# Attention with beacons and a max-out layer: the opening's steps in a new order

## The chip, the cores and the metric

The kernel runs on one core of one Trainium2 chip. That core has five engines, each with a program of its own that it works through in order: TensorE (PE in the profile; its weight loads have a row of their own, PEld), VectorE (DVE), ScalarE (ACT), GpSimd (POOL) and SyncE (SP). [...] Transfers between the device memory and the on-chip memory are issued by an instruction on SP, ACT or POOL and then run by themselves on 16 DMA engines; SP's and ACT's are called hardware-generated in the profile (queues q1 and q10), POOL's software-generated (q0). The metric is the device time of one execution in microseconds (us); lower is better.

## What is computed

Attention for 8 batches and 8 heads over 576 tokens with 64 values per head, with 16 beacon keys and values put in front of every head, and then a feed-forward layer with the maximum of three products:

```
k_all = concatenate([beacon_k, k]); v_all = concatenate([beacon_v, v])
scores = (q @ k_all.T) / sqrt(64)        # causal over the 576 tokens, beacons always seen
a = softmax(scores); x = a @ v_all       # heads side by side: 4608 tokens x 512
h = max(x @ w1, x @ w2, x @ w3)          # 512 x 768 each
out = h @ w_out                          # 768 x 512
```

## The kernel before

**Pairs, quads, halves.** The 64 heads of all batches are handled as 32 pairs; a batch has four (pairs 0 to 3 are batch 0). Two pairs make a quad: quad 0 is pairs 0 and 1, quad 1 is pairs 2 and 3. For batch 0 the 576 tokens are also cut in two halves of 288, so that the first half can be loaded, turned and used before the second is there.

**What a pair goes through.** Its q and k are loaded with tokens on the partitions, cast to bf16, turned on PE by transposes against an identity (`turn_half`, line 428, transposes in line 440; `turn` for whole pairs, lines 384 to 402), and copied from PSUM into `qT` and `kT` (line 448, or `evac_q` and `evac_k`, lines 452 to 467). The beacon keys of batch 0 are loaded apart ("load keys 0", line 351), cast (line 864), turned (`turn_beacons`, line 356) and copied into the first 16 columns of `kT`: for pair 0 directly (line 366), for all pairs by way of `bT` (line 367), from which "keys" (`place_beacons`, line 460) copies them for one pair. "scores p g" (`emit_scores`, line 503) issues the products of one of four groups of key tiles (line 514) and one ACT exponential over all of them (line 523). "mask p g" zeroes what lies above the diagonal, on POOL by an affine select (line 542) or on DVE by a product with a triangle (line 540). "values quad half" (`emit_pv`, line 561) multiplies with a column of ones and with v (line 583); "invert" and "multiply" divide by the sums (lines 604, 606 and 616) and write `xT`.

**The feed-forward part.** "ffn" (`mm1_halves`, line 634) multiplies a block of `xT` with one of the three weights, 8 matmuls of 256 columns (line 638), and DVE takes the result, by a copy for the first weight (line 630) and by a maximum for the others (line 632). In the opening the weights are used in their order, three steps each: the first three "ffn" steps with last argument 0 need the first weight, the next three the second, the last three the third. Each weight is loaded by POOL in two DMAs that cast on the way ("load w", line 338), the first with the rows for quad 0, the second with those for quad 1.

**Loads of the first batch.** Pairs 0 and 1, first half: q and k apart, from SP or ACT as the list says ("load half", line 223), cast by an engine (line 231). Pairs 2 and 3, first half, and all second halves: by POOL with a cast on the way, two pairs at once ("load quad half", line 240; `("load quad half", 1, 0)` is pairs 2 and 3, first half, `(0, 1)` pairs 0 and 1, second half). "load quad" does the same for pairs 4 to 7 (line 249), "load pair" loads pairs 8 and 9 by SP. "load v0 t" (line 298) loads tile t of batch 0's v by SP; where an engine is named, that engine first writes one word of the tile (line 301), so that SP can't issue the load before that engine has come so far. "cast v0 t" casts it (line 328).

**Filler.** PE runs matmuls of no use in three forms: "busy n cols" (`keep_busy`, line 482) n matmuls of a constant tile; the last argument of "scores" and "values" (`spare`, line 476) so many of 320 columns ahead of the step; the last two arguments of "half" (`fill`, line 404) so many pairs of transposes ahead of the turn, in the order idle for k, then idle_q for q. All are in PE's program, so they take their time even if the step behind them could go ahead.

**The order of the work** is written out by hand in two lists, `first_steps` (lines 901 to 1074) and `loop_steps` (from line 1075), which are emitted one after the other. Every step issues its instructions, DMAs too, to the end of the programs of the engines that it uses. `first_steps` handles batch 0 and most of batch 1; `loop_steps` the rest.

## Time and profile before

| What | Value |
|---|---|
| Time, median of three runs (lowest to highest) | 285.1 us (284.79 to 286.19) |
| The profiled execution's own time | 285.21 us |
| Its span, first to last instruction | 283.3 us |
| PE busy | 276.3 us, 98% of the span |
| DVE, ACT, POOL busy | 176.5, 154.5, 143.4 us |
| Loaded and stored | 35.13 MB read, 9.44 MB written |

The time of an execution is 1.9 us longer than its span; that part lies before the first and behind the last instruction. A busy PE is not a PE that does useful work: filler counts as busy. The page's chain of waits follows the end of the execution back to its start; the tables by stage show how busy each engine is in a stretch of time; the timeline lists instructions in order of start with the idle time before them and what ended it; the list of DMA issues tells for each how long it took from issue to landing.

### The profile page before, as it was taken

To read this page: it belongs to the slowest core of one execution; us is meant where nothing else is said; L and a number is where in the kernel's file an instruction comes from. 1 tells how busy PE (TensorE), PEld (TensorE's weight loads), DVE (VectorE), ACT (ScalarE), POOL (GpSimd) and SP (SyncE) were. 2 spreads that over 40 slices of the span, in tenths; PEclk is the share of its full clock that TensorE was granted. 3 is DMA by queue.
4 is the path that set the end of the run, shared out by engine and by line. 5 is a ranking of instruction groups with operands and counts; after the bars stand their busy time and mean duration, and the time that the engine had idled before them with its cause. 6 is when DMAs were issued, how large, how long until landed. Compare 5 with 4: busy or idle time off the path is not lost.

```text
span 283.3 us, 11781 instructions
## 1 busy us (share of the span) xinstructions
PE 276.3 (98%) x5099; PEld 201.5 (71%) x5099; DVE 176.5 (62%) x331; ACT 154.5 (55%) x249; POOL 143.4 (51%) x316
## 2 busy tenths in 40 slices
PE   8999999999999999999999999999999999999995
PEld 7666777757777576768677686767877687757762
DVE  2456777886676765756566666646575665661754
ACT  2876676897563574637464574725765474624000
POOL 4462318898741583758734497508854682400000
PEclk9999999999999999999999999999999999999999
DMA  9999999999978399999999969989999962003004
GB/s 153 168 171 206 223 234 157 247 206 309 211 141 168 45 252 178 171 197 147 189 178 215 236 91 176 166 204 185 217 160 170 163 177 76 2 3 150 2 2 185
DMA packets 118307, 46.27 MB, mean 163 GB/s; under 512 B 107248, under 2 KB 112880, under 8 KB 118256
## 3 DMA queue, kind: packets, MB, share of 16 engines
q1 hardware_dynamic: 111888, 39.20, 75.6%
q0 software_dynamic: 5808, 6.00, 13.0%
q8 instruction: 40, 0.66, 1.1%
q10 hardware_dynamic: 560, 0.33, 0.4%
q14 instruction: 11, 0.09, 0.1%
HBM read 35.13 MB, written 9.44 MB: 157 GB/s over the span
## 4 chain that ended last, share of the span: by engine, by line
PE 91%; DMA 3%; ACT 2%; POOL 1%; DVE 1%; issue 1%; ACTq 0%; POOLq 0%
PE t L700 44%; PE t L726 16%; PE t L583 11%; PE t L514 6%; DMA quad<-in_k_dram 3%; PE pv L478 2%; ACT at_sb L523 2%; PE pv L638 2%; PE sc L514 1%; PE sc L638 1%; PE fps L638 1%; PE t L398 1%; POOL at_sb L542 1%; PE wide L583 1%; PE pv L583 1%
## 5 line engine op out<-in xcount | busy, mean ns | idle before, releaser
L700 PE MATMUL t<-xT,w_sb 64*128 64x288 bf16 (+1 forms) x1008 | 129.6, 285 | 0.0
L700 PE MATMUL t<-xC,wC 64*128 64x288 bf16 (+1 forms) x1008 | 129.6, 285 | 0.0
L523 ACT ACTIVATE at_sb<-t 128x992 bf16<-128x992 f32 (+1 forms) x96 | 82.6, 863 | 42.8 <-PE t L514 37.1
L632 DVE TENSOR_TENSOR hT<-hT,t 128x576 bf16<-128x576 bf16 (+1 forms) x84 | 63.7, 763 | 30.6 <-PE t L700 30.6
L542 POOL TENSOR_SCALAR_AFFINE_SELECT at_sb<-at_sb 128x256 bf16<-128x256 bf16 (+2 forms) x143 | 53.6, 390 | 53.7 <-ACT at_sb L523 41.2
L700 PEld LDWEIGHTS <-w_sb 64*128 64x128 bf16 x1008 | 51.3, 94 | 12.6 <-issue 1.1
L700 PEld LDWEIGHTS <-wC 64*128 64x128 bf16 x1008 | 51.0, 94 | 12.4
L726 PE MATMUL t<-w_out_sb,hT 128*128 128x512 bf16 x210 | 47.9, 380 | 0.0
L681 POOL COPY xC<-xT 64x576 bf16<-64x576 bf16 (+1 forms) x26 | 18.0, 693 | 42.8 <-DVE xT L616 42.5
L630 DVE CAST hT<-t 128x576 bf16<-128x576 f32 (+1 forms) x36 | 27.7, 769 | 14.8 <-PE t L700 14.6
L726 PEld LDWEIGHTS <-hT 128*128 128x128 bf16 x210 | 19.3, 98 | 22.8 <-issue 0.9
L259 POOL CAST p<-st 96x768 bf16<-96x768 f32 x44 | 34.9, 822 | 0.3
L734 DVE COPY y<-t 128x1024 f32<-128x1024 f32 (+1 forms) x20 | 21.8, 1091 | 20.5 <-PE t L726 20.3
L514 PE MATMUL t<-qT,kT 64*128 64x288 bf16 (+4 forms) x288 | 33.1, 279 | 0.0
L616 DVE TENSOR_TENSOR xT<-t,recip 128x288 bf16<-128x288 f32 (+2 forms) x78 | 22.9, 351 | 16.0 <-ACT recip L606 10.7
L604 ACT ACTIVATE lnd<-t 128x288 f32<-128x288 f32 x26 | 10.7, 410 | 36.9 <-PE t L583 36.9
L514 PEld LDWEIGHTS <-kT 64*128 64x128 bf16 x400 | 18.5, 94 | 11.4 <-issue 6.7
L583 PEld LDWEIGHTS <-v_sb 128*32 128x32 bf16 (+1 forms) x1408 | 24.6, 96 | 1.6 <-issue 0.4
L523 ACT ACTIVATE at_sb<-sc 128x736 bf16<-128x736 f32 (+5 forms) x28 | 23.2, 862 | 4.2 <-PE sc L514 4.1
L583 PE MATMUL t<-at_sb,v_sb 128*32 128x96 bf16 (+8 forms) x1144 | 23.3, 228 | 0.0
L316 POOL CAST v_sb<-st 128x1536 bf16<-128x1536 f32 (+2 forms) x21 | 18.4, 894 | 0.6 <-DMA st<-in_v_dram 0.6
L583 PEld LDWEIGHTS <-ones 128*32 128x32 bf16 (+2 forms) x512 | 10.9, 95 | 6.7 <-issue 3.9
(125 smaller groups left out, 220.1 us busy)
## 6 DMA issues: line engine op xcount, KB each, us to landing
out_dram<-y SPq DMA_DIRECT2D x15, 512.0 KB, 4.6
st<-in_q_dram SPq DMA_DIRECT2D x24, 288.0 KB, 5.8
st<-in_k_dram SPq DMA_DIRECT2D x24, 288.0 KB, 6.2
st<-in_v_dram SPq DMA_DIRECT2D x24, 256.0 KB, 5.5
w_sb<-in_moe_w_dram POOLq DMA_DIRECT2D x6, 384.0 KB, 8.9
st<-in_v_dram SPq DMA_DIRECT2D x8, 224.0 KB, 5.1
st<-in_v_dram SPq DMA_DIRECT2D x8, 160.0 KB, 4.7
out_dram<-y SPq DMA_DIRECT2D x5, 256.0 KB, 4.6
```

What stands on the lines that cost most here:

```text
L259: cast(t16.rearrange("p r h d -> p h r d"), st[0:QP, i * NQ2 : (i + 1) * NQ2].rearrange("p (h r d) -> p h r d", h=2, r=QR),)
L316: cast(v_sb[0:n, t:t1].rearrange("p t h d -> p (t h d)"), st[0:n, (t - t_lo) * H * D : (t1 - t_lo) * H * D],)
L514: nc.tensor.matmul(ps[:, e, off : off + q1 - q0], kT[hs, 128 * t : 128 * t + 128], qT[hs, q0:q1], start=True, stop=True, tile_position=(64 ...
L523: nc.scalar.activation(out=both_heads(p, gi), in_=ps[:, :, 0 : g_width(p, gi)], func=AF.Exp, scale=scale)
L542: nc.gpsimd.affine_select(out=view, in_=view, compare_op=ALU.is_ge, fill=0.0, base=x0, pattern=[[0, 2], [1, hi - lo]], channel_multiplier=-1,)
L583: nc.tensor.matmul(ps[bank][32 * j : 32 * j + 32, lo + q0 - qa : lo + qb - qa], lhsT, at_view(PPQ * quad + j // 2, t, j % 2, q0, qb), star ...
L616: nc.vector.tensor_mul(xT[:, 2 * g + part - 1, c0 + ca : c0 + cb], ps[bank][:, lo : lo + cb - ca], recip[:, ca:cb],)
L630: (by_i or by_dve)(h, ps)
L632: nc.vector.tensor_max(h, h, ps)
L700: nc.tensor.matmul(ps[:, e], w[own(e), ct, cols], x, start=(ct == 0 and not over), stop=(ct == n_ct - 1 and over), tile_position=(64 * e, 0),)
L726: nc.tensor.matmul(ps[:, u], h_tile(tt + u, ft), w_out_sb[:, ft, :], start=(ft == 0), stop=(ft == n_ft - 1),)
L734: nc.vector.tensor_copy(y[:, 0:n], ps[:, 0:n])
```

## The change

Only `first_steps` changes; every function and the whole of `loop_steps` stay. Every operation on data is still done, once. What differs is the order, the queue or engine of some steps, and the filler:

- q of pair 0 goes from SP to ACT, q of pair 1 from ACT to SP. ACT's queue issues q of pair 0, the beacon keys, k of pair 0 and k of pair 1, in this order. SP's issues q of pair 1 alone.
- The first filler is 40 matmuls of 64 columns and 12 of 174, instead of 27 of 200 and 16 of 160.
- The triangle is made later, behind the first beacon copy on POOL.
- PE turns pair 0, the beacon keys, pair 3 and then pair 1, where it turned the beacon keys, pair 0, pair 1, pair 3; scores of pair 1 come first, then pair 0, pair 2, pair 3.
- Casts, masks and beacon copies go to other engines in many places, and the later loads by POOL and SP stand at other places in the order.

The diff, with its core; what is left out moves steps of the same kinds between the places shown:

```
 first_steps = [
-    ("load half", 0, 0, "sp"),
-    ("busy", 27, 200),
+    ("load half", 0, 0, "act"),
+    ("load keys 0", "act"),
     ("identity",),
-    ("busy", 16, 160),
-    ("triangle",),
+    ("load half", 0, 1, "act"),
     ("load quad half", 1, 0),
-    ("load half", 1, 0, "act"),
-    ("load half", 0, 1, "act"),
-    ("cast half", 0, 1, "dve"),
-    ("load keys 0", "act"),
+    ("busy", 40, 64),
+    ("busy", 12, 174),
+    ("load half", 1, 0, "sp"),
+    ("load half", 1, 1, "act"),
+    ("cast half", 0, 0, "dve"),
+    ("cast half", 0, 1, "act"),
     ("cast keys 0", "act"),
-    ("load half", 1, 1, "sp"),
-    ("cast half", 0, 0, "act"),
-    ("turn keys 0",),
+    ("half", 0, 0, "ffn", "act", 0, 0),
     ("cast half", 1, 0, "pool"),
     ("load v0", 0, "pool"),
+    ("turn keys 0",),
     ("cast half", 1, 1, "dve"),
-    ("load v0", 1, "pool"),
-    ("half", 0, 0, "ffn", "act", 0, 8),
-    ("keys", 1, "act"),
-    ("load v0", 2),
-    ("half", 1, 0, "pv", "act", 3, 5),
+    ("load v0", 1),
+    ("load v0", 2, "pool"),
     ("keys", 3, "pool"),
+    ("half", 3, 0, "ffn", "dve", 0, 0),
+    ("triangle",),
+    ("keys", 1, "dve"),
+    ("half", 1, 0, "pv", "act", 0, 0),
+    ("cast v0", 0, "dve"),
+    ("scores", 1, 0, 4),
     ("load quad half", 0, 1),
+    ("load w", 0),
+    ("half", 2, 0, "pv", "dve", 6, 8),
+    ("keys", 2, "pool"),
+    ("mask", 1, 0, "pool"),
     ("scores", 0, 0, 0),
-    ("scores", 1, 0, 0),
-    ("load w", 0),
-    ("half", 3, 0, "ffn", "dve", 0, 0),
-    ("half", 2, 0, "pv", "dve", 4, 0),
-    ("mask", 1, 0, "dve"),
-    ("cast v0", 0, "pool"),
     ("cast v0", 1, "act"),
+    ("mask", 0, 0, "dve"),
+    ("scores", 2, 0, 0),
+    ("cast v0", 2, "dve"),
     ("scores", 3, 0, 0),
-    ("mask", 0, 0, "dve"),
+    ("mask", 2, 0, "dve"),
+    ("values", 0, 0, "pv", 0, 4, 0),
     ("load v0", 3, "dve"),
-    ("keys", 2, "pool"),
-    ("cast v0", 2, "act"),
-    ("scores", 2, 0, 7),
-    ("values", 0, 0, "pv", 0, 4, 0),
     ("half", 0, 1, "ffn", "act", 0, 9),
     ("invert",),
-    ("mask", 3, 0, "dve"),
     ("multiply",),
-    ("scores", 0, 2, 4),
-    ("mask", 2, 0, "pool"),
+    ("scores", 0, 2, 3),
+    ("mask", 3, 0, "pool"),
     ("load keys 1",),
     ("scores", 0, 3, 0),
     ("values", 1, 0, "ffn", 0, 4, 0),
     ("load quad half", 1, 1),
     ("invert",),
+    ("load v0", 4, "dve"),
+    ("half", 1, 1, "pv", "act", 1, 0),
+    ("mask", 0, 2, "dve"),
     ("multiply",),
-    ("mask", 0, 2, "pool"),
     ("scores", 0, 1, 0),
-    ("half", 1, 1, "pv", "act", 1, 0),
-    ("load v0", 4, "dve"),
-    ("scores", 1, 2, 4),
+    ("scores", 1, 2, 7),
+    ("ffn", "ffn", 0),
     ("mask", 0, 1, "pool"),
-    ("cast v0", 3, "act"),
+    ("scores", 1, 1, 0),
+    ("scores", 1, 3, 0),
+    ("cast v0", 3, "dve"),
+    ("ffn", "ffn", 0),
+    ("load w", 1),
+    ("half", 2, 1, "pv", "dve", 0, 0),
     ("ffn", "ring", 0),
-    ("ffn", "ffn", 0),
+    ("mask", 1, 1, "pool"),
+    ("scores", 2, 3, 0),
+    ("half", 3, 1, "pv", "act", 4, 0),
+    ("mask", 1, 3, "dve"),
+    ("cast keys 1", "act"),
+    ("scores", 2, 2, 3),
     ("mask", 1, 2, "dve"),
-    ("scores", 1, 3, 0),
-    ("scores", 1, 1, 0),
-    ("half", 2, 1, "pv", "dve", 0, 0),
-    ("mask", 1, 3, "dve"),
-    ("ffn", "ffn", 0),
-    ("half", 3, 1, "pv", "dve", 0, 0),
-    ("load v", 1, 0, "dve"),
+    ("mask", 0, 3, "dve"),
+    ("mask", 2, 3, "dve"),
+    ("scores", 3, 2, 0),
     ("cast v0", 4, "dve"),
-    ("mask", 0, 3, "dve"),
-    ("mask", 1, 1, "dve"),
-    ("scores", 2, 3, 0),
-    ("scores", 2, 2, 7),
-    ("load w", 1),
-    ("scores", 3, 2, 0),
-    ("mask", 2, 3, "dve"),
-    ("cast keys 1", "dve"),
     ("values", 0, 1, "pv", 0, 4, 0),
+    ("invert",),
     ("turn keys 1",),
-    ("invert",),
     ("scores", 3, 3, 0),
     ("ffn", "ffn", 0),
+    ("scores", 2, 1, 0),
+    ("keys", 5, "dve"),
     ("load quad", 1, 0),
+    ("load v", 1, 0, "dve"),
+    ("mask", 3, 3, "dve"),
+    ("load pair", 8, "pool"),
+    ("ffn", "ffn", 0),
+    ("multiply",),
+    ("mask", 3, 2, "pool"),
+    ("load pair", 9, "dve"),
     ("load w", 2),
-    ("mask", 3, 3, "dve"),
-    ("multiply",),
-    ("load pair", 9, "pool"),
-    ("scores", 2, 1, 0),
-    ("mask", 2, 2, "pool"),
-    ("ffn", "ffn", 0),
     ("mask", 2, 1, "pool"),
     ("scores", 3, 1, 0),
-    ("keys", 6, "dve"),
-    ("keys", 4, "pool"),
+    ("mask", 3, 1, "pool"),
     ("ffn", "ring", 0),
-    ("mask", 3, 1, "dve"),
-    ("keys", 5, "dve"),
-    ("mask", 3, 2, "pool"),
+    ("mask", 2, 2, "pool"),
     ("whole", 4, "ffn", "dve"),
+    ("keys", 6, "act"),
     ("values", 1, 1, "pv+", 0, 4, 0),
 ...
```

Of what is left out, the main things are these: the "mask" steps behind this point stay on POOL or DVE in slightly different places; `("load w_out", "pool")` becomes `("load w_out", "dve")`; and several "scores" and "ffn" steps of pairs 4 to 7 change places with their neighbours.

More of the change, by code (lines that the diff above doesn't have):

```diff
@@ L999 @@
-        ("mask", 3, 2, "pool"),
+        ("mask", 2, 2, "pool"),
         ("whole", 4, "ffn", "dve"),
+        ("keys", 6, "act"),
         ("values", 1, 1, "pv+", 0, 4, 0),
         ("invert",),
+        ("keys", 4, "dve"),
         ("scores", 4, 1, 0),
@@ L1007 @@
         ("whole", 5, "ring", "act"),
-        ("load pair", 8),
         ("ffn", "ring", 1),
-        ("mask", 4, 1, "dve"),
         ("ffn", "ring", 1),
         ("scores", 5, 0, 0),
-        ("mask", 5, 0, "dve"),
-        ("ffn", "pv", 1),
-        ("load v", 1, 1),
-        ("scores", 4, 0, 0),
-        ("scores", 4, 3, 0),
-        ("ffn", "ring", 0),
-        ("ffn", "pv", 1),
-        ("load quad", 1, 1),
-        ("mask", 4, 2, "dve"),
-        ("scores", 5, 1, 0),
-        ("keys", 7, "act"),
-        ("scores", 5, 2, 0),
-        ("scores", 5, 3, 0),
-        ("mask", 4, 3, "pool"),
-        ("ffn", "pv", 0),
-        ("whole", 6, "ring", "dve"),
-        ("cast v", 1, 0),
+        ("scores", 4, 3, 0),
+        ("ffn", "pv", 1),
+        ("scores", 4, 0, 0),
+        ("load v", 1, 1),
+        ("keys", 7, "dve"),
+        ("scores", 5, 1, 0),
+        ("mask", 4, 1, "dve"),
+        ("ffn", "pv", 1),
+        ("ffn", "ring", 0),
+        ("mask", 5, 0, "dve"),
+        ("scores", 5, 2, 0),
+        ("mask", 4, 2, "dve"),
+        ("load quad", 1, 1),
+        ("scores", 5, 3, 0),
+        ("ffn", "pv", 0),
+        ("cast v", 1, 0),
+        ("mask", 4, 3, "pool"),
+        ("whole", 6, "ring", "act"),
+        ("ffn", "ring", 0),
         ("mask", 5, 3, "pool"),
-        ("load w_out", "pool"),
+        ("mask", 5, 1, "dve"),
         ("mask", 4, 0, "pool"),
-        ("ffn", "ring", 0),
+        ("load w_out", "dve"),
         ("mask", 5, 2, "pool"),
@@ L1037 @@
         ("scores", 6, 0, 0),
-        ("mask", 5, 1, "pool"),
+        ("mask", 6, 0, "pool"),
         ("scores", 6, 2, 0),
@@ L1044 @@
         ("load", 1, "pool"),
-        ("mask", 6, 0, "pool"),
-        ("load", 2, "pool"),
         ("ffn", "pv", 1),
@@ L1049 @@
         ("multiply",),
-        ("keys", 8, "pool"),
+        ("load", 2, "pool"),
+        ("cast pair", 8),
+        ("scores", 7, 1, 0),
         ("load", 1),
-        ("cast pair", 8),
+        ("scores", 6, 3, 0),
+        ("whole", 8, "pv", "dve"),
+        ("mask", 6, 3, "dve"),
+        ("keys", 8, "act"),
         ("cast v", 1, 1),
-        ("scores", 6, 3, 0),
+        ("scores", 7, 0, 0),
         ("scores", 7, 2, 0),
         ("cast pair", 9),
-        ("whole", 8, "pv", "dve"),
-        ("mask", 6, 3, "dve"),
-        ("scores", 7, 0, 0),
-        ("scores", 7, 1, 0),
         ("mask", 7, 1, "pool"),
+        ("mask", 7, 2, "pool"),
         ("values", 2, 1, "ring", 0, 4, 0),
-        ("mask", 7, 2, "pool"),
+        ("keys", 9, "act"),
         ("invert",),
         ("scores", 7, 3, 0),
+        ("mask", 7, 3, "pool"),
         ("whole", 9, "ring", "act"),
+        ("multiply",),
+        ("mask", 6, 2, "pool"),
+        ("ffn", "pv", 1),
         ("mask", 6, 1, "pool"),
-        ("mask", 7, 3, "pool"),
-        ("multiply",),
         ("mask", 7, 0, "pool"),
-        ("keys", 9, "act"),
-        ("ffn", "pv", 1),
-        ("mask", 6, 2, "pool"),
     ]
```

## The prediction, made before the change was run

> **What bounds the kernel now.** I read the table by stages first, for where PE is short of work.

> ```profile
> 5.00:10.00 5.00, 4.70 (x111) 3.98 (x110) 1.54 (x4) 3.00 (x8) 1.87 (x4) 1.00 1.37 187
> 10.00:15.00 5.00, 4.54 (x121) 3.10 (x116) 2.69 (x12) 4.19 (x7) 2.46 (x8) 1.00 1.11 144
> 15.00:20.00 5.00, 4.44 (x84) 2.48 (x83) 3.07 (x12) 4.51 (x10) 2.73 (x7) 1.00 1.15 194
> 20.00:25.00 5.00, 4.44 (x57) 3.12 (x56) 3.37 (x8) 2.67 (x5) 2.94 (x6) 1.00 0.98 183
> 25.00:30.00 5.00, 5.00 (x114) 3.62 (x113) 2.69 (x11) 3.75 (x8) 0.32 (x1) 1.00 1.22 205
> ...
> 150.00:200.00 50.00, 50.00 (x914) 36.49 (x910) 30.84 (x50) 25.88 (x41) 28.18 (x68) 1.00 1.07 185
> ```

> The second column is the stretch, the third PE's busy time; the last three are granted clock, DMA share and GB/s. From 25 us on PE never stops (50.00 of 50.00 later). So what the opening wins or loses by the time the weights flow is the gain or loss of the whole kernel. Between 5 and 25 us PE idles 0.30 + 0.46 + 0.56 + 0.56 = 1.9 us, and it also runs filler. I then followed the timeline for what it waits for.

> ```profile
> 6.25 0.62 ACT L864 CAST bk<-bk 16x512 bf16<-16x512 f32 x1 [4.15 <-DMA bk<-in_beacon_k_dram]
> ...
> 8.75 0.40 PE L514 MATMUL sc<-qT,kT 64*128 64x288 bf16 x6
> ...
> 9.18 1.94 ACT L523 ACTIVATE at_sb<-sc 128x1024 bf16<-128x1024 f32 x2 [0.30 <-PE sc L514]
> ...
> 11.33 1.13 PE L478 MATMUL sc<-busy 128*128 128x320 bf16 x7
> ...
> 12.94 1.05 ACT L523 ACTIVATE at_sb<-sc 128x1024 bf16<-128x1024 f32 x1
> ...
> 14.06 0.95 POOL L542 TENSOR_SCALAR_AFFINE_SELECT at_sb<-at_sb 128x224 bf16<-128x224 bf16 x3 [2.54 <-ACT at_sb L523]
> ...
> 15.65 0.69 POOL L240 DMA_DIRECT2D quad<-in_k_dram  x1
> ...
> 18.76 0.39 ACT L448 COPY qT<-pv 128x288 bf16<-128x288 bf16 x1
> ...
> 18.93 0.41 POOL L542 TENSOR_SCALAR_AFFINE_SELECT at_sb<-at_sb 128x256 bf16<-128x256 bf16 x1 [1.89 <-ACT at_sb L523]
> ...
> 19.28 1.10 POOL L338 DMA_DIRECT2D w_sb<-in_moe_w_dram  x2
> ...
> 19.83 1.43 PEld L638 LDWEIGHTS <-w_sb 128*128 128x128 bf16 x14 [0.25 <-DMA w_sb<-in_moe_w_dram]
> ...
> 22.79 0.32 PE L440 MATMUL pv<-ident,quad 96*64 96x96 bf16 x6 [0.56 <-DMA quad<-in_k_dram]
> ```

> ```profile
> 28.09 1.05 PE L638 MATMUL fps<-xT,w_sb 128*128 128x256 bf16 x8
> ```

> ```profile
> w_sb<-in_moe_w_dram POOLq DMA_DIRECT2D x1, 384.0 KB, 7.8
> ...
> w_sb<-in_moe_w_dram POOLq DMA_DIRECT2D x2, 384.0 KB, 8.7
> ...
> quad<-in_k_dram POOLq DMA_DIRECT2D x1, 144.0 KB, 7.1
> ...
> w_sb<-in_moe_w_dram POOLq DMA_DIRECT2D x1, 384.0 KB, 8.2
> ```

> Up to 14 us the chain is key loads, casts, turns, then four first exponentials on ACT (two from 9.18, the last ending at 13.99). Then three landings of POOL's queue gate PE, one after the other. **Gate 1**: the second half of the first weight; its issue begins half of 1.11 behind 9.65 (row below), at 10.2, and lands at 10.2 + 9.6 = 19.8 (9.6 since the two halves have the median 8.7 and the first took 7.8). PE waits 0.25 us. **Gate 2**: k of pairs 2 and 3, second half, 15.65 + 7.1 = 22.75; PE waits 0.56. **Gate 3**: the second half of the second weight, issued at 19.28 + 0.55 = 19.83, landing 8.2 later at 28.03; PE needs it at its third matmul behind 28.09, about 28.3, and isn't stopped. The change can win only what these gates let through.

> **The change, part by part.** *First filler.*

> ```profile
> L478 PE MATMUL pv<-busy 128*128 128x200 bf16 x27 | 4.5, 364 | 1.3 <-DVE busy L138 1.3
> L478 PE MATMUL pv<-busy 128*128 128x160 bf16 x16 | 1.3, 232 | 0.1
> ```

> Columns: the group, its busy time and the mean of one, the idle time before it. The first 27 cost 4.5 / 27 = 0.167 us for 200 columns, 0.83 ns a column; the next 16 cost 0.081 for 160, 0.51 ns. So PE starts slow and gets fast some 4.5 us after its start. At the slow rate the new stream takes 40 x 64 x 0.83 + 12 x 174 x 0.83 = 2.1 + 1.7 = 3.9 us and ends at 1.3 + 3.9 = 5.2 instead of 7.2. That alone wins nothing: PE then waits for keys.

> *Loads.*

> ```profile
> 1.29 0.47 ACTq L223 DMA_DIRECT2D h<-in_k_dram  x1
> ...
> 1.79 0.47 ACTq L351 DMA_DIRECT2D bk<-in_beacon_k_dram  x1
> ...
> 5.70 0.63 DVE L231 CAST h<-h 96x384 bf16<-96x384 f32 x2 [3.89 <-DMA h<-in_k_dram]
> ...
> 6.77 0.51 ACT L231 CAST h<-h 96x384 bf16<-96x384 f32 x1
> ...
> 7.31 0.53 PE L408 MATMUL fps<-ident,busy 96*64 96x96 bf16 x16
> ...
> 8.14 0.46 DVE L448 COPY kT<-fps 128x288 bf16<-128x288 bf16 x1 [1.82 <-PE fps L440]
> ...
> 8.33 0.67 POOL L240 DMA_DIRECT2D quad<-in_q_dram  x1 [0.28 <-issue]
> ...
> 9.65 1.11 POOL L338 DMA_DIRECT2D w_sb<-in_moe_w_dram  x2
> ```

> ```profile
> 31.32 0.19 DVE L460 COPY kT<-bT 128x16 bf16<-128x16 bf16 x1
> ```

> ```profile
> h<-in_q_dram SPq DMA_DIRECT2D x1, 144.0 KB, 3.0
> ...
> h<-in_k_dram SPq DMA_DIRECT2D x1, 144.0 KB, 3.7
> ...
> h<-in_k_dram ACTq DMA_DIRECT2D x1, 144.0 KB, 4.4
> ...
> bk<-in_beacon_k_dram ACTq DMA_DIRECT2D x1, 32.0 KB, 4.4
> ```

> Before, k of pair 0 landed at 1.29 + 4.4 = 5.7 and the beacon keys at 6.2. Now k of pair 0 is third on ACT, with 32 KB more ahead of it. It can't be priced from one row: below, 5.7 (the same bytes are in flight on all queues); above, 1.0 later, two steps of 0.5 as from the third issue to the fourth landing. I take 5.9, nearer to the 0.5 that 32 KB cost on this queue less the place that SP's shorter queue frees. k of pair 1, fourth, follows by between 0.5 (the beacon keys) and 1.2 us: 6.8. The four issues take 0.5 each from about 0.8, so the last leaves at 2.3; nothing else is due on ACT then, and q's moves between SP and ACT are covered by the later k.

> *To the first scores.* k of pair 0: 5.9 + ACT's cast 0.51 = 6.4; turning 0.4 (12 of the 16 transposes of 0.53) to 6.8. From there DVE is the chain: copy of pair 0's k 0.46, cast of pair 1's k 0.35, both copies of pair 3 0.92, beacons 0.19, copy of pair 1's k 0.46: 9.2. The beacon keys' cast (0.62 behind 6.4) and turn are hidden under this; they would show if they passed 8.5. First scores at 9.25 instead of 8.75, **+0.5**, with one pair more turned (0.4 us of PE).

> *ACT's four exponentials.* The first starts 0.43 behind its scores (8.75 to 9.18), at 9.7. Between the first and second scores PE now has pair 2's 12 transposes and 28 of filler, 40 x 0.033 = 1.3, which I round down to 1.1 since 0.53 holds the tail of the last. Second scores at 10.65, exponential 11.1 to 12.0; then one cast of v (0.6, as the beacons' 512 columns; the other cast left for DVE, which has room) and two exponentials of 0.97: 14.5 instead of 13.99, **+0.5**. POOL's mask and the issue of pairs 2 and 3's second half follow: k at 16.1 instead of 15.65.

> *Gate 1.* POOL's issues now stand behind the beacon copy and the triangle (two instructions, each under the 0.41 of the mask at 18.93). Beacons at about 7.8, triangle to 8.4, so the quad at 8.4 instead of 8.33 and the weight at 9.75: 19.9 instead of 19.8. v's first tiles are released earlier, which may give 0.2 back. Bounds -0.4 and +0.7.

> *Gate 2.* The +0.5 at its issue is hidden while the first weight, ahead in the same queue, is in flight to 19.8. With that cover gone it would cost the 0.5. I take 0.1: 22.85.

> *Gate 3.* On ACT the copy of pair 1's q (0.39, at 18.76) now stands ahead of the exponential whose mask at 18.93 holds back the second weight. **+0.4**: issue 19.68, second half 28.4. Against it, SP's last v tile is asked for earlier and will be out of the way: bounds -0.4 and +0.5.

> *Filler behind the first scores.* Matmuls of 320 columns fall from 22 to 13: 9 x 0.16 (1.13 / 7) = -1.4. Filler transposes rise from 28 to 56: 28 x 0.033 = +0.9. Net -0.5; but gates 1 and 2 both stand behind most of it. At gate 2 both orders have done the same work (two of the first weight's steps, all of pair 1's scores), so PE leaves it at 23.1 in both, and between gates 2 and 3 the new order has 4 matmuls and 8 transposes where the old has 7: about 0.3 shorter. PE is at the second weight at 27.8 instead of 28.09 and waits to 28.4 where it needed the half at 28.3: **+0.1**.

> *Steps moved further down.*

> ```profile
> 39.29 1.05 PE L638 MATMUL wide<-xT,w_sb 128*128 128x256 bf16 x8
> ```

> The third weight's issue now waits on POOL for a mask of pair 3, about 28; with 1.1 to issue and 8.2 to land it is there at 37.3, 2.0 ahead of this first use. Pairs 4 to 7's loads wait for masks too, but queue behind the second weight anyway. Masks and v casts that change engine go to DVE, busy for 2.69 and 3.37 of 5.00 us from 10 and 20 us: hidden, unless v's fourth tile, whose load is released later, holds DVE; I allow +0.3. The later beacon keys' cast waits on ACT instead of DVE, without a taker until 28. Behind 28 us both orders do the same PE work in nearly the same order.

> **Sum**: +0.1, of -0.6 (gate 3 lower bound, filler saved) to +0.7. The profiled execution took 285.21 (span 283.3 and 1.9 around it), 0.1 above the median; so 285.2 on the scale of the median.

> **The rivals.**

> *The clock stays low.* The stream now ends at 5.2, and pair 0's q turns by 5.5; PE then stands still till 6.4. The rows above show the fast rate only about 4.5 us into a stream without a hole, at about 5.8. If PE is still slow from 6.4 to 12, the four filler matmuls ahead of the first scores cost 4 x (320 x 0.83 ns - 0.15) = 0.5, two score groups 2 x 0.4 and the 40 transposes 1.2 more: 2.4 us. The covers take some 0.4: **287.2**. For it: 3.9 us of work is less than the 4.5 that it took. Against it: the hole is one of 0.9 us. It decides from the point at which the hole keeps the clock low past 6.4. [...]

> *Keys late.* Pair 0's k lands at 6.7, pair 1's at 7.9, since 464 KB now leave by one queue. Scores, POOL's quad and the weight shift by 0.8 to 1.1, and gate 1 with them: **286.2**. For it: landing grew by 0.7 from SP's first to its second load. Against: all queues shared the same engines before.

> *The gates open early.* If loads run freer, the idle 0.46 + 0.56 + 0.56 of 10 to 25 us goes with the 0.5 of filler, 2.1 at most, some 1.5 likely: **283.6**. For it: SP's loads stand elsewhere, and 0.3 less filler lies between the last gates. Against: the weights' issue is no earlier.

> **How the numbers follow.** No change to speak of, 285.2 (284.5 to 285.9): 0.58. Clock 0.13, keys late 0.13, gates early 0.16. About 0.5%, 1.4 us, is what a measurement here tells from no change: below 283.7 faster, above 286.5 slower. Faster: 0.10 of the gates' case. Slower: 0.12 of the clock's and 0.05 of the keys'. The range, 283.8 to 286.8, leaves out about 0.09 at each end.

> **What would show it.** First filler over by 5.2; k of pair 0 cast at 5.9; first scores at 9.25; fourth exponential over at 14.5; PE waiting at the first weight, at pairs 2 and 3's k near 22.8, and at the second weight near 28.4. Wrong if the 320-column filler at 9 us runs at 0.27 us each, if a gate moved by over 0.7 us, or if PE waits for a mask or copy behind 30 us.

## The result: slower by about 1%, outside the forecast

| | Before | Changed |
|---|---|---|
| Time, median (lowest to highest of 6 executions each) | 285.31 us (284.79 to 286.41) | 288.67 us (287.19 to 290.73) |
| Profiled execution, and its span | 285.21, 283.3 us | 289.22, 287.5 us |

The ratio is 1.0109, with a 95% interval of 1.0066 to 1.0153. An execution over 1.5% above the fastest of its kernel counts in the median but not in the ratio. The forecast was 285.2 us, of a range that ended at 286.8, so the likeliest case and the range both missed. The rival that the clock stays low came true and explains one part of the loss; another part comes from a place of which the prediction said nothing.

The table by stages of the changed kernel, with the columns as before:

```profile
5.00:10.00 5.00, 4.49 (x53) 2.70 (x52) 2.45 (x7) 2.00 (x6) 2.47 (x6) 1.00 1.36 223
10.00:15.00 5.00, 4.50 (x80) 3.09 (x80) 1.84 (x6) 3.38 (x5) 1.93 (x6) 1.00 1.21 167
15.00:20.00 5.00, 5.00 (x87) 2.82 (x91) 2.05 (x9) 3.12 (x7) 2.27 (x5) 1.00 0.91 159
20.00:25.00 5.00, 5.00 (x81) 3.05 (x74) 2.30 (x7) 3.77 (x7) 1.47 (x3) 1.00 0.58 80
25.00:30.00 5.00, 4.84 (x114) 3.43 (x115) 3.56 (x11) 3.62 (x7) 1.82 (x4) 1.00 1.00 181
```

PE is busier than before from 15 to 25 us, 5.00 of 5.00 in both stages. That looks like a gain and is none. From 5 to 15 us it gets through 53 + 80 matmuls where it did 111 + 121. And between 20 and 25 us the transfers have fallen to 80 GB/s from 183: PE no longer waits for loads, since it is itself so late that the masks and buffers that let the loads go come late too.

The timeline of PE in the changed kernel (start, duration, group, count, and in brackets the idle time before and what ended it):

```profile
1.34 4.27 PE L478 MATMUL pv<-busy 128*128 128x64 bf16 x52 [1.34 <-DVE busy L138]
...
6.20 0.45 PE L440 MATMUL fps<-ident,h 96*64 96x96 bf16 x6 [0.21 <-ACT h L231]
...
7.67 0.45 PE L440 MATMUL fps<-ident,quad 96*64 96x96 bf16 x6 [0.21 <-DMA quad<-in_k_dram]
...
8.53 1.25 PE L478 MATMUL sc<-busy 128*128 128x320 bf16 x4
...
13.72 0.61 PE L514 MATMUL sc<-qT,kT 64*128 64x288 bf16 x6 [0.40 <-ACT at_sb L523]
...
21.69 1.12 PE L478 MATMUL sc<-busy 128*128 128x320 bf16 x7
```

The filler of 320 columns is the clock's gauge in this kernel. At 8.53 us four of them take 1.25 us, 0.3 each with the tail of the last; at 21.69 us seven take 1.12, the 0.16 of before. In between six scores take 0.61 where they took 0.40 at 8.75 before. So PE runs slow to about 20 us. The trace's record of the clock begins at 20.48 us, with the rise: the 32 matmuls with v that start at 14.92 take 1.40 us, the 32 that start at 19.83 take 1.19, those behind them run fast. The column of the granted clock says 1.00 in all of these stages: **the low rate ahead of the first rise does not show in it**, and has to be read from the duration of a matmul of known shape.

What hangs on PE and ACT in the mixed timeline of the same execution:

```profile
5.63 0.51 ACT L231 CAST h<-h 96x384 bf16<-96x384 f32 x1 [3.53 <-DMA h<-in_k_dram]
...
9.71 0.61 PE L514 MATMUL sc<-qT,kT 64*128 64x288 bf16 x6
...
14.07 1.94 ACT L523 ACTIVATE at_sb<-sc 128x1024 bf16<-128x1024 f32 x2
...
17.66 0.69 POOL L240 DMA_DIRECT2D quad<-in_k_dram  x1
...
23.35 1.12 POOL L338 DMA_DIRECT2D w_sb<-in_moe_w_dram  x2
```

```profile
30.64 1.05 PE L638 MATMUL fps<-xT,w_sb 128*128 128x256 bf16 x8
```

The keys came as forecast (cast at 5.63, forecast 5.9). The fourth exponential is over at 14.07 + 1.94 = 16.0 instead of 13.99, the second half of pairs 2 and 3 leaves at 17.66 instead of 15.65, the second weight at 23.35 instead of 19.28, and its first product stands at 30.64 instead of 28.09.

**Where the time goes, by landmarks of PE.** For the kernels of this study I took the start of the first product with the first weight, of the first scores of the loop (the first group in tile `t`), of the first product with w_out, and the span:

| Kernel | First weight | Loop | w_out | Span |
|---|---|---|---|---|
| before | 19.47 | 55.45 | 58.26 | 283.3 |
| changed | 23.01 | 57.72 | 62.13 | 287.5 |
| new order, old filler | 19.79 | 55.90 | 60.76 | 285.8 |
| old order, new filler | 21.58 | 56.73 | 59.53 | 284.8 |
| new order, transposes in the hole | 20.08 | 56.02 | 62.67 | 288.3 |
| new order, 23 fillers of 200 | 23.75 | 62.27 | 67.23 | 292.4 |
| new order, 15 long fillers | 22.58 | 57.80 | 60.97 | 286.9 |
| changed, once more | 22.73 | 58.70 | 62.45 | 287.6 |
| old order, w_out late | 19.36 | 55.88 | 59.73 | 284.7 |
| new order, old filler, w_out early | 19.43 | 57.03 | 60.97 | 286.1 |
| changed, w_out early | 23.11 | 59.71 | 62.52 | 288.2 |

In the changed kernel PE loses 3.54 us up to the first weight. It gets 1.27 back by 57 us, about as much as the old order waited there (0.25 and 0.56 us for transfers, 0.42 for a copy at 34.44 us), and then loses 1.60 more in the short stretch from the loop's first scores to w_out. Up to w_out it is 3.87 late, of 4.2 in all. So there are two losses to explain: one ahead of 20 us, one between 57 and 62.

### The profile page after: what moved, and what is told of

It is laid out like the page before. It is cut to its first block, busy times and chain, and to the rows that moved or that the text cites. A ratio compares the mean times of both kernels' runs of the same rounds, so it can differ in the third digit from the quotient of the medians.

```text
span 287.5 us, 11762 instructions
## 1 busy us (share of the span) xinstructions
PE 279.0 (97%) x5085; PEld 201.2 (70%) x5099; DVE 176.2 (61%) x331; ACT 155.2 (54%) x250; POOL 144.2 (50%) x315
## 3 DMA queue, kind: packets, MB, share of 16 engines
HBM read 35.13 MB, written 9.44 MB: 155 GB/s over the span
## 4 chain that ended last, share of the span: by engine, by line
PE 94%; DMA 2%; issue 1%; ACT 1%; DVE 1%; POOL 0%; POOLq 0%
PE t L700 44%; PE t L726 16%; PE t L583 11%; PE t L514 6%; PE sc L514 3%; PE pv L638 3%; PE pv L583 2%; DMA quad<-in_k_dram 2%; PE sc L638 2%; PE fps L638 1%; PE sc L478 1%; PE t L398 1%; ACT at_sb L523 1%; PE fps L583 1%; PE pv L440 1%
## 5 line engine op out<-in xcount | busy, mean ns | idle before, releaser
L523 ACT ACTIVATE at_sb<-t 128x992 bf16<-128x992 f32 (+1 forms) x96 | 82.6, 863 | 43.0 <-PE t L514 37.2
L632 DVE TENSOR_TENSOR hT<-hT,t 128x576 bf16<-128x576 bf16 (+1 forms) x84 | 63.6, 763 | 30.6 <-PE t L700 30.6
L542 POOL TENSOR_SCALAR_AFFINE_SELECT at_sb<-at_sb 128x256 bf16<-128x256 bf16 (+2 forms) x146 | 54.9, 391 | 48.2 <-ACT at_sb L523 44.8
L726 PE MATMUL t<-w_out_sb,hT 128*128 128x512 bf16 x196 | 47.2, 380 | 0.7
L681 POOL COPY xC<-xT 64x576 bf16<-64x576 bf16 (+1 forms) x26 | 18.2, 700 | 43.9 <-DVE xT L616 43.7
L514 PE MATMUL t<-qT,kT 64*128 64x288 bf16 (+4 forms) x288 | 33.0, 279 | 0.1
L514 PEld LDWEIGHTS <-kT 64*128 64x128 bf16 x400 | 18.5, 96 | 12.2 <-issue 5.4
L523 ACT ACTIVATE at_sb<-sc 128x992 bf16<-128x992 f32 (+5 forms) x27 | 22.7, 873 | 6.6 <-PE sc L514 6.6
## 6 DMA issues: line engine op xcount, KB each, us to landing
w_sb<-in_moe_w_dram POOLq DMA_DIRECT2D x6, 384.0 KB, 6.8
```

Of the source, the lines that this page charges most:

```text
L514: nc.tensor.matmul(ps[:, e, off : off + q1 - q0], kT[hs, 128 * t : 128 * t + 128], qT[hs, q0:q1], start=True, stop=True, tile_position=(64 ...
L523: nc.scalar.activation(out=both_heads(p, gi), in_=ps[:, :, 0 : g_width(p, gi)], func=AF.Exp, scale=scale)
L542: nc.gpsimd.affine_select(out=view, in_=view, compare_op=ALU.is_ge, fill=0.0, base=x0, pattern=[[0, 2], [1, hi - lo]], channel_multiplier=-1,)
L632: nc.vector.tensor_max(h, h, ps)
L726: nc.tensor.matmul(ps[:, u], h_tile(tt + u, ft), w_out_sb[:, ft, :], start=(ft == 0), stop=(ft == n_ft - 1),)
```

## The experiments

**Theory one, the clock.** In the changed kernel the rise at 20.48 us stands at the end of 3.41 us in which PE was full (busy 3.41 of 3.41 from 17.07). The theory: PE gets its full rate only at the end of such a stretch, one with next to no hole. The old filler runs to 7.2 us without one; the new one ends at 5.6, and the turns behind it wait for keys. **Rival:** the new order holds up queues whatever the clock, or the small size of the 64-column matmuls is to blame.

### new_order_old_filler and old_order_new_filler: the two halves of the change apart

```
 # new_order_old_filler: the changed kernel with
-        ("busy", 40, 64),
-        ("busy", 12, 174),
+        ("busy", 27, 200),
+        ("busy", 16, 160),
 # old_order_new_filler: the kernel before with
-    ("busy", 27, 200),
+    ("busy", 40, 64),
-    ("busy", 16, 160),
+    ("busy", 12, 174),
```

> The changed kernel with the first filler of the kernel before (27 matmuls of 200 columns and 16 of 160). Clock theory (the changed kernel loses because its short first filler leaves PE at the slow rate until about 20 us): 320-column filler at 9 us at 0.15 us each, time 284.7 to 285.7, ratio to before 0.998 to 1.002. Order theory (the new order of loads, turns and scores itself costs the time): 288 or more, ratio 1.008 and up.

> The kernel before with the changed kernel's first filler (40 matmuls of 64 columns and 12 of 174), the order untouched. Clock theory: PE stands still from 5.3 to about 7 us, then runs at the slow rate far past 10 us; time 287.5 to 289.5. Order theory: 284.5 to 286, as before.

Measured: new order with the old filler 287.72 us, ratio 1.0078 (1.0049 to 1.0106), between the two theories; old order with the new filler 287.23, ratio 1.0061 (1.0037 to 1.0084), a little under the clock theory's range. The timeline of PE in the first:

```profile
7.27 0.45 PE L440 MATMUL fps<-ident,h 96*64 96x96 bf16 x12
...
8.80 0.32 PE L440 MATMUL fps<-ident,quad 96*64 96x96 bf16 x6 [0.40 <-DMA quad<-in_k_dram]
...
9.30 0.72 PE L478 MATMUL sc<-busy 128*128 128x320 bf16 x4
```

and in the second:

```profile
6.92 0.27 PE L360 MATMUL sc<-ident,bk 16*128 16x16 bf16 x4 [1.31 <-ACT bk L864]
...
12.76 1.80 PE L478 MATMUL sc<-busy 128*128 128x320 bf16 x7
```

With the old filler PE is fast at 9.30 (0.72 for four) in spite of the new order, and the landmarks up to the loop are 0.32 and 0.45 us behind the old order's: that is what the order alone costs there, and it lies within the forecast's -0.6 to +0.7. With the new filler even the old order stands still for 1.31 us and runs slow past 12.76 (1.80 for seven, 0.26 each). So the filler sets the clock, in either order. But each half alone already costs about 2 us, and the first has its fast clock and still loses: 2.81 us from loop to w_out has become 4.86. Theory one explains the loss ahead of 20 us, not the one behind 55. What the clock costs in the whole time is not settled by the medians: the old filler takes back 0.95 of the 288.67 us, and the intervals of the two ratios overlap.

### new_order_23x200: is it the size of the matmuls?

```
-        ("busy", 40, 64),
-        ("busy", 12, 174),
+        ("busy", 23, 200),
```

> The changed kernel with 23 matmuls of 200 columns as its first filler: the same 3.9 us of work as 40 of 64 and 12 of 174. If it is the length of the stream and the hole behind it that keep the rate low, this is slow too, 288 to 289.5. If it is the small size of the 64-column matmuls, the rate rises by 7 us and the time is 284.7 to 286.

Measured: 294.11 us, ratio 1.0287 (1.0241 to 1.0334). The filler of old size but short ends no later than the changed kernel's, the hole behind it is 1.47 us, since k of pair 0 came late in this execution, and PE is slow to about 20 us again. It isn't the 64-column shape. That it is so much worse than the changed kernel was not expected: by the landmarks 4.4 us more than there go between the first weight and w_out. In that stretch PE waits 2.42 us for a copy of q until 40.91, the granted clock falls to 0.50 behind that wait, from 41.03 to 44.45, and the hole shown below is 0.60 longer than the changed kernel's. What made the copy late was not tried.

### new_order_transposes_in_hole: does a transpose keep the clock up?

```
-    ("half", 0, 0, "ffn", "act", 0, 0),
+    ("half", 0, 0, "ffn", "act", 20, 0),
```

> The changed kernel with 20 pairs of filler transposes put between the turns of pair 0's q and k (some 2.1 us at the slow rate, from 5.9 to 8.0 us), so that PE has no hole there. If transposes count as work for the clock, the rate rises by about 8 us and the time is 285 to 286.5, the first scores at most 1 us later. If they don't count, PE stays slow to 15 us or more and the time is 289 to 291.

Measured: 292.12 us, ratio 1.0221 (1.0178 to 1.0264), above what either case gave. The timeline of PE in the profiled execution, which took 290.06:

```profile
5.78 1.13 PE L408 MATMUL fps<-ident,busy 96*64 96x96 bf16 x40
...
8.57 0.72 PE L478 MATMUL sc<-busy 128*128 128x320 bf16 x4
```

The forty transposes fill the hole, and PE is fast at 8.57: 0.72 us for the four that took 1.25. The rise itself, at 6.03 us, can't be credited to them: in a later execution of the unaltered changed kernel (below) the rate rises at 5.87 without them. What they show is that the rate stays. From 6.03 to 9.44 PE is busy 2.76 of 3.41 us here, of which only 0.79 lie outside transposes, and the rate is kept. In the run with 15 long fillers (below) it is busy 2.43 from 5.97 to 9.39, with 0.78 outside transposes, and the rate is lost at the end. **So transposes do count as work for the clock here.** The two runs show it for transposes done as a product with an identity.

The first weight's product is at 20.08, the loop at 56.02, only 0.57 behind before. And yet the median is the second worst of all, since 6.65 us pass from the loop to w_out. So a clock that is up in the opening doesn't remove the second loss. This holds for the profiled execution, the fastest of six; the other five have mean granted clocks of 0.988 to 0.994, so in them the rate fell again somewhere.

**Theory two, the second loss.** In four of these kernels PE has a hole between the loop and w_out, or just ahead of the loop, that the profile puts down to "issue", that is to nothing that it records. These are the lines of PE at that place in the changed kernel,

```profile
60.21 0.47 PE L583 MATMUL t<-at_sb,v_sb 128*32 128x176 bf16 x24 [1.38 <-issue]
```

with the old filler,

```profile
56.65 0.47 PE L583 MATMUL t<-at_sb,v_sb 128*32 128x288 bf16 x16
58.99 0.33 PE L583 MATMUL t<-at_sb,v_sb 128*32 128x80 bf16 x16 [1.87 <-issue]
```

with the transposes in the hole,

```profile
54.29 1.80 PE L638 MATMUL pv<-xT,w_sb 128*128 128x256 bf16 x15 [0.56 <-issue]
...
62.41 0.33 PE L583 MATMUL t<-at_sb,v_sb 128*32 128x96 bf16 x13 [3.64 <-issue]
```

and with 23 fillers of 200 columns:

```profile
65.73 0.56 PE L583 MATMUL t<-at_sb,ones 128*32 128x288 bf16 x16 [1.98 <-issue]
```

The table of queues on the page of the changed kernel has the candidate (packets, MB, share of 16 engines):

```profile
q8 instruction: 40, 0.66, 1.0%
```

The changed kernel's program gives PE 5099 matmuls and as many weight loads, 10198 instructions. The 40 packets hold 16 KB each; if all are PE's, that is 255 instructions to a packet on the mean. Blocks of 256 are my estimate from these counts; the program makes 39.8 of them. Theory two: **PE stands still since its next block of instructions has not arrived.** I then thought that w_out's load, which the new order issues 3.7 us later (POOL, 48.32 instead of 44.66, behind a cast that waits for v of batch 1), was what delays the packet. Rival: something else in the new order's loop start.

### old_order_w_out_late, new_order_longer_filler, new_order_longer_filler_values_early

```
 # old_order_w_out_late: the kernel before with
-    ("load w_out", "pool"),
     ... seven steps
     ("mask", 5, 1, "pool"),
+    ("load w_out", "pool"),
 # new_order_longer_filler: the changed kernel with
-        ("busy", 12, 174),
+        ("busy", 15, 174),
 # new_order_longer_filler_values_early: that, and
     ("half", 3, 1, "pv", "act", 4, 0),
+    ("load v", 1, 0, "dve"),
     ...
     ("keys", 5, "dve"),
     ("load quad", 1, 0),
-    ("load v", 1, 0, "dve"),
```

> The order before with one step moved: the load of w_out stands seven steps later on GpSimd, behind the last mask of batch 1, so that it is issued at about 47 us instead of 44.7. Theory of the late instruction block: the packet of the instruction queue that lands at 53 us in the kernel before lands at 55 to 57, a hole of 1 to 1.5 us put down to issue opens in the values of pair 3 at the loop's start, and the time is 286.3 to 286.8 us. Rival (w_out's transfer has no part in the hole): no hole, and 285.2 us as before.

> The new opening with 15 instead of 12 of the long warming matmuls (40 of 64 columns, then 15 of 174), so that the filler lasts until the turn of pair 0 can start. Clock theory (the rate rises only at the end of a stretch of about 3.4 us, here at about 6.1 us from the span's start, that has no hole of 0.2 us or more on TensorE): the first four scores take 0.15 us each instead of 0.27, the first scores still come at 9.2 to 9.8 us, the second weight's first product comes at 28.3 to 28.8 us instead of 30.6, and the time falls from 288.7 to 286.7 to 287.5 us: the hole in the values of pair 3 at the loop's start stays, since the keys still stand ahead of the values of batch 1. Rival (the new order by itself holds the queues up, whatever the clock): scores at the slow rate or not, the second weight's first product stays behind 30 us and the time within 0.6 us of the changed kernel's 288.7.

> As the run with 15 long warming matmuls, and the load and cast of batch 1's first values moved up to stand right behind the half of pair 3, batch 1, as near to where the order before had them as the new order allows. Theory of the late instruction block: the cast of these values on GpSimd ends by 42 to 43 us instead of 43.9 to 45.5, the load of w_out is issued by 45 instead of 46.8 to 48.3, TensorE's 16 KB of instructions land by 54 us, the hole put down to issue in the values of pair 3 (1.38 in the changed kernel, 1.87 with the old filler) is gone, and the time is 285.0 to 285.7 us. Rival (the hole comes of something else in the new order's loop start): the hole of 1 to 2 us stays and the time is that of the run beside it, 286.7 to 287.5.

Old order with w_out late: 286.49 us, ratio 1.0034 (1.0014 to 1.0053), in the range that theory two gave. The step moved less than expected, to 45.82 us instead of 47, and with that the trace has a hole, smaller than expected, where the one of before had none:

```profile
57.79 0.48 PE L583 MATMUL t<-at_sb,v_sb 128*32 128x176 bf16 x24 [0.80 <-issue]
```

The packet of the instruction queue moved from the half microsecond at 53.0 to that at 55.0.

New order with the longer filler: 288.64 us, ratio 1.010 (1.006 to 1.014), no gain. The second weight's first product is at 30.21. Both numbers are the rival's, that the new order holds the queues up whatever the clock; but the clock was not repaired, so the run can't decide for it. The filler ends at 6.0 us without a hole, but:

```profile
6.79 0.32 PE L440 MATMUL fps<-ident,h 96*64 96x96 bf16 x6 [0.50 <-ACT h L231]
...
8.68 0.72 PE L478 MATMUL sc<-busy 128*128 128x320 bf16 x4
9.49 0.61 PE L514 MATMUL sc<-qT,kT 64*128 64x288 bf16 x6
```

The rate goes up (0.72) and **comes down again** before the first scores (0.61 instead of 0.40): the turns behind the filler have holes of 0.50, 0.20 and 0.26 us. This time the granted clock has it (0.50), since the fall is recorded here where the rate that had not yet risen was not (1.00 in the changed kernel):

```profile
5.97:9.39 3.42, 2.43 (x45) 1.50 (x44) 2.03 (x6) 2.01 (x6) 1.28 (x5) 1.00 1.40 227
9.39:12.80 3.41, 3.22 (x57) 2.47 (x58) 1.50 (x4) 1.40 (x2) 2.85 (x7) 0.50 1.26 149
```

The second column behind the stretch is PE's busy time, 2.43 of 3.42; the granted clock falls to 0.50 at 9.39. With the old filler PE is busy 2.77 and 2.72 in the stretches from 5.98 and 9.39 and stays fast. So in this order the filler has to reach into the waits of the turns (the old one, to 7.2 us, does), and three matmuls more don't do it.

With the values early as well: 291.74 us, ratio 1.0149 (1.0104 to 1.0194), not better than without, and outside what both cases gave. Its executions spread from 288.04 to 294.36 us and the profiled one took 292.52, so its trace stands for few of them and is not used here. The time was not repaired, and what the run was to show stays open.

The longer filler's trace holds the best evidence for theory two, though:

```profile
59.02 0.51 PE L583 MATMUL t<-at_sb,v_sb 128*32 128x176 bf16 x28 [0.19 <-issue]
59.35 0.68 PE L583 MATMUL t<-at_sb,ones 128*32 128x288 bf16 x20
59.85 1.19 PE L583 MATMUL t<-at_sb,v_sb 128*32 128x288 bf16 x56
60.97 2.76 PE L726 MATMUL t<-w_out_sb,hT 128*128 128x512 bf16 x12
63.57 0.68 PE L398 MATMUL t<-ident,p 96*128 96x96 bf16 x12
64.95 2.75 PE L726 MATMUL t<-w_out_sb,hT 128*128 128x512 bf16 x12 [0.70 <-PE t L398]
```

From the first hole to the next there are 28 + 20 + 56 + 12 + 12 = 128 matmuls: with their weight loads 256 instructions, one block of the size estimated above. And the place of the hole follows the number of instructions ahead of it. The changed kernel has 52 filler matmuls, and its hole is behind the 7th matmul with v of the loop's first values. With 55 fillers it is behind the 4th, with 43 behind the 16th, with 23 behind the 36th (32 with v and 4 with ones), each shifted by exactly the filler matmuls added or taken. With 40 transposes more it moves up by 40, out of this group, to the hole of 0.56; the next block's end, 15 + 6 + 12 + 32 + 20 + 43 = 128 matmuls later, falls behind the 43rd with v of the second half, where the hole of 3.64 is. The hole follows the count of instructions in these runs, whatever data stands there, so I read it as a wait for instructions and count this as shown. The 256 from hole to hole agree with the 255 to a packet, and the holes of these kernels came to 0.19 to 3.64 us.

### new_order_old_filler_w_out_early, new_order_w_out_early, changed_again

```
 # both: the kernel named, with
+    ("load w_out", "dve"),
     ("cast v", 1, 0),
     ("mask", 4, 3, "pool"),
     ...
-    ("load w_out", "dve"),
```

> The new order with the filler of before, and the load of w_out moved up from behind three masks to ahead of the cast of batch 1's first values on GpSimd, so that it no longer waits for that cast. Theory of the late instruction block: w_out is issued by 44 us instead of 46.8, the instruction queue's packet lands at 53 to 54 us instead of 56, the hole put down to issue in the values of pair 3 (1.87 us with w_out late) shrinks below 0.3, and the time is 285.6 to 286.3 us instead of 287.7. Rival (the whole traffic around 45 us sets the packet, not w_out alone): the hole stays above 1 us and the time stays at 287.2 to 288.2.

> The changed kernel with its own short filler, and only the load of w_out moved up ahead of the cast of batch 1's first values. The low rate up to 20 us stays, so the start of the loop stays near 57.7 us; theory of the late instruction block: w_out is issued by 46 us instead of 48.3, the hole of 1.38 us in the values of pair 3 falls below 0.3, and the time falls from 288.7 to 287.1 to 287.7 us. Rival: the hole stays above 1 us and the time within 0.5 us of 288.7.

> The changed kernel once more, unaltered, for a second profiled execution. If the stretches at whose end the rate can rise stand at the same times after the start in every execution, the scores of pair 3 at about 8.5 us again take 0.27 us each and the rate rises at about 20 us. If they stand elsewhere from execution to execution, the rise comes at another time, and that alone can spread the times of the changed kernel (287.2 to 290.7) wider than those of the kernel before (284.8 to 286.4), whose filler is long enough for every such stretch.

With the old filler and w_out early: 288.5 us, ratio 1.0094 (1.0065 to 1.0123), not faster than the 287.72 without. w_out left at 44.58 us, as in the kernel before, and the packet still landed in the half microsecond at 56.0; a hole of 0.93 stayed, with another of 0.93 at 35.89, which is 384 matmuls, three blocks, ahead of it. **So my cause for the late packet fell**: w_out's late issue may open the hole (in the old order), but its early issue doesn't close it. In the changed kernel with w_out early (median 290.93 us) the profiled execution has no hole; but its loop starts at 59.71, 1 to 2 us later than in the two profiles without the move, so the packet of 58.2 is in time. Its ratio of 1.0067 (1.0026 to 1.0108) does not differ clearly from the changed kernel's, and its executions spread from 286.2 to 292.9; I draw nothing from it.

The changed kernel once more took 289.27 us (profiled before: 289.22). The same program, the same time, and another history of the clock. The hole is at the same matmul, but 0.71 us long instead of 1.38, so the size of a hole in one trace is not exact evidence, the 0.80 with w_out late included. PE's timeline:

```profile
6.41 0.32 PE L440 MATMUL fps<-ident,h 96*64 96x96 bf16 x6 [0.42 <-ACT h L231]
...
8.38 0.32 PE L440 MATMUL fps<-ident,quad 96*64 96x96 bf16 x6 [0.84 <-DMA quad<-in_k_dram]
8.88 0.90 PE L478 MATMUL sc<-busy 128*128 128x320 bf16 x4
```

and its granted clock, in tenths of a microsecond (third number from the end):

```profile
9.20:9.30 0.10, 0.10 (x2) 0.07 (x1) 0.10 (x2) 0.06 (x1) 0.10 (x1) 0.89 1.45 220
9.30:9.40 0.10, 0.10 (x3) 0.00 (x0) 0.10 (x1) 0.00 (x0) 0.10 (x1) 0.50 1.39 215
...
19.50:19.60 0.10, 0.10 (x8) 0.00 (x0) 0.08 (x1) 0.10 (x1) 0.00 (x0) 0.91 1.40 175
19.60:19.70 0.10, 0.10 (x10) 0.07 (x4) 0.06 (x1) 0.10 (x1) 0.00 (x0) 1.00 1.47 195
```

Here the rate was up at 6.41 us (0.32 for six transposes, not 0.45), fell at 9.28 and rose at 19.52. The stretch of 10.24 us is three times 3.41. With the longer filler the granted clock was low for as long, from 9.39 to 19.63 us, and with 23 fillers for a third of that, from 41.03 to 44.45. So in these traces both edges follow a window of 3.41 us. In one execution of this kernel a window ends at 5.87, just behind the filler, in the other at 6.83, so it is chance whether the early rise is had. It won nothing here: k of pair 3 came later, PE waited 0.84 us for it instead of 0.21, and the first scores stand at 9.72 instead of 9.71. From 9.3 to 19.5 us the rate was low in both.

How full must a window be? PE's busy time (the second column behind the stretch) doesn't tell. These are windows of the old order with w_out late, at whose end the rate rose, and of the new order with the old filler, which kept it:

```profile
1.19:4.60 3.41, 3.26 (x20) 2.99 (x21) 0.62 (x14) 0.91 (x1) 2.47 (x6) 1.00 0.82 194
```

```profile
57.18:60.59 3.41, 1.60 (x88) 1.58 (x91) 2.44 (x3) 1.88 (x4) 3.28 (x5) 1.00 1.23 199
```

So 3.26 brought the rate in one kernel where 3.35 did not in another (the changed kernel from 13.65, below), and 1.60 kept it where 2.43 lost it. Counting the columns of the matmuls, each weighted with its matmul's size as the profile prints it, as a share of 128*128, the largest here (96*64 for a transpose in L440), sorts the windows better. The windows are laid out from each trace's first rise in steps of 3.41 us. In the eleven traces of the table, up to the last 8 us, the three windows that lost the rate have 1376, 2048 and 2548 such columns and all that kept it 2956 or more. The slow ones that did not bring it have at most 2928, and those that did 3160 or more, but for the changed kernel's with 2904. Some 2900 in 3.41 us is my estimate of the border, from these counts.

## Why the prediction was wrong

- **Keys, casts, copies: right.** k of pair 0 was cast at 5.63 (forecast 5.9), the last copy for the first scores was done at 9.10 (9.2), and the rival that the keys come late, one queue having more bytes, did not happen in this execution (in the run with 23 fillers, with the same loads, k of pair 0 was cast at 6.64). The first scores came at 9.71 instead of 9.25, behind four slow filler matmuls that PE ran first.
- **What the order costs by itself: right in size up to the loop.** +0.1, of -0.6 to +0.7, was forecast; with the clock repaired by the old filler it is +0.45 where the loop begins. The gates were less exact. With the old filler PE waits for k of pairs 2 and 3 until 23.86 us, a full 1.0 later than forecast for gate 2:

```profile
23.86 0.32 PE L440 MATMUL pv<-ident,quad 96*64 96x96 bf16 x6 [0.78 <-DMA quad<-in_k_dram]
```

- **The shorter filler at no cost: the first step that failed.** The sum has no term for the clock; it says of the filler's earlier end "That alone wins nothing: PE then waits for keys", and prices all that follows at the fast rate. The forecast's own rival had the mechanism, that the hole behind the short filler keeps the rate low, but gave it a chance of 0.13, with "the hole is one of 0.9 us" as evidence against, and let it end at 12 us. The hole behind the filler came to 0.21 in the profiled execution, and the low rate lasted to 20 us. The changed kernel by the windows that end with its rise (PE's busy time behind the comma):

```profile
3.41:6.83 3.42, 3.08 (x33) 2.33 (x30) 0.49 (x2) 1.20 (x3) 0.82 (x3) 1.00 1.20 181
6.83:10.24 3.41, 3.18 (x38) 1.87 (x37) 2.31 (x7) 0.81 (x4) 2.71 (x7) 1.00 1.37 231
10.24:13.65 3.41, 2.97 (x56) 2.36 (x53) 0.91 (x2) 2.03 (x3) 1.69 (x5) 1.00 1.24 152
13.65:17.07 3.42, 3.35 (x72) 2.10 (x73) 1.57 (x8) 2.36 (x4) 0.99 (x4) 1.00 0.83 157
17.07:20.48 3.41, 3.41 (x49) 1.47 (x44) 1.40 (x5) 2.48 (x5) 1.28 (x2) 1.00 1.13 178
```

  Turns and scores leave idle time in each of them up to 17.07 us; only the last is full (3.41 of 3.41), and at its end the rate rises. So the four exponentials ended 2.0 late, not 0.5, and the second weight was asked for 4.1 late, not 0.4.
- **The price of that rival: about right, by luck.** It added 2.0 us (287.2). By the loop's start the changed kernel is 2.27 late, of which the order alone has 0.45 by the run with the old filler, so some 1.8 are left for the clock. But the rival had the low rate end at 12 us, which gave 2.4, and 0.4 taken back. At the first weight the runs have 3.54 less 0.32, that is 3.2, and the opening takes back 1.27. The two errors cancel. The end should have been looked for in a full window; the stages of before, which lack 0.30, 0.46 and 0.56 us of PE up to 20 us, show none by 12 us.
- **"Behind 28 us both orders do the same PE work in nearly the same order": the second step that failed.** They do, and yet the loop's start costs 1.60 us more in the changed kernel and 2.05 more with the old filler, for a block of instructions that comes later. Packets and holes fit: PE goes on 2.7 to 2.8 us behind the start of the packet (57.37 and 60.21 changed, 56.30 and 58.99 old filler, 55.12 and 57.79 w_out late). In the kernel before the packet is at 53.20, and PE comes to the 7th matmul with v at 56.33, so that it was in time by a few tenths only.
- **The gates that open early: no.** PE's waits for loads went, as that rival had it, but because PE itself was late.

What the runs leave open: which transfer holds the instruction packet back. From the block's end before it (128 matmuls earlier, by counting back: 51.24 us before, 53.50 changed, 52.05 old filler) to the packet it is 2.0 us in the kernel before and 3.9 and 4.2 in the others, if the packet is asked for at that point, which no record shows. The DMA share is 1.14 there in the kernel before and 1.15 in the changed one, and 1.14 from 50 to 56 us with the old filler; by that mean all 16 engines are taken. Why the hole in the run with transposes is as long as 3.64 us was not tried either. Nor was it tried which of the moved steps makes the order's 0.45. No version here beats the kernel before, and the sum of what is understood (a fast clock and no hole would leave the new order 0.45 behind) gives no reason to expect one.

## What to carry to other kernels

Here the filler that reached past the first waits of the real work, to 7.2 us, kept the rate up, and those that only filled the time until that work could start, to 5.6 and 6.0 us, did not. My estimate from this for other kernels: find the first stretch behind the warming matmuls in which PE stays full for the 3.41 us measured here, and price the slow rate at least up to there (20.48 us in the changed kernel). Since the windows stood elsewhere in each of its two traces (one ended at 6.83 us, in the other at 5.87), an early rise in one trace is no proof. Read the rate from the duration of a matmul of known shape (0.3 us against 0.16 for 320 columns), since the granted clock stayed at 1.00 until the first fall. Where short matmuls stood densely (128 of them in 5 us), an "issue" hole that moved with the count of instructions was here a program that arrived late, and the change paid for it (1.38 us) even where it left the work alone.
